# Retention and gated MLP on one core: smaller, paced loads, one mask product per first chunk, and another written order

## The chip, the cores and the metric

The kernel runs on one core of one Trainium2 chip. The time is that of the core on the device, in microseconds (us), from one execution of the whole program; the figure given for a kernel is the median of several executions. A core has a matrix engine (TensorE, PE in the profile, with its weight loads as PEld), a vector engine (VectorE, DVE), an activation engine (ScalarE, ACT), a general engine (GpSimd, POOL) and a sequencer for transfers (SyncE, SP). Each runs its own list of instructions in order and waits on the others by semaphores. Sixteen DMA engines move data between the chip's main memory (HBM) and the core's on-chip memory (SBUF); the matrix engine writes its products into a second on-chip memory (PSUM).

## The reference

There are 4 batches, 8 heads, 768 tokens and 64 dimensions per head. The first half is a retention layer, in which a state per head decays with every token:

```python
gamma = 1.0 - 2.0 ** (-5.0 - np.arange(H, dtype=np.float32))
for t in range(S):
    state = gamma[None, :, None, None] * state + np.einsum('bhd,bhe->bhde', k[:, :, t], v[:, :, t])
    y[:, :, t] = scale * np.einsum('bhd,bhde->bhe', q[:, :, t], state)
```

Its output, with the heads side by side (512 columns), is `x` of the second half, in which a causal convolution of 5 taps gives a gate:

```python
for k in range(K):
    gate_pre += conv_w[k][None, None, :] * xp[:, k:k + S, :]
gate = 1.0 / (1.0 + np.exp(-gate_pre))
val = x @ w_val
return (gate * val @ w_out).astype(np.float32)
```

The two weight matrices and the taps come in as 64-bit numbers, which the kernel turns into 32-bit ones itself.

## The kernel before

**Tiling.** The tokens are cut into 6 chunks of 128. A "visit" is one chunk of one batch, so there are 24, numbered `g`, with the 4 batches of a chunk in a row: visits 0 to 3 are the first chunk. The input of a visit is one block of 1 MB in four parts of 0.25 MB: part 0 the queries by dimension, part 1 the keys by dimension, part 2 the values by token, part 3 the keys by token. `load(g, part)` (L322) brings a block, or some of its parts, into one of four buffers (`LB`, L22), named `att` in the trace. A line of one partition has 2 KB for each part.

**The first chunk** (visits 0 to 3) needs no state from earlier. For each visit PE makes the scores (`first_scores`, L357, letter `s`), DVE multiplies them with a mask table (`first_mask`, L393), PE multiplies the masked scores with the values (`first_y`, L436, letter `y`), DVE scales the result into `x` (`evac`, L501). ACT then rounds `x` to `xh` (L512) and POOL makes the rest `xl` (L516). The two mask tables (one for each half `x` of the heads) are made once, by two DVE and two ACT instructions (`first_table`, L379), from `small_sb`, a block of 68 KB. Separately the keys by token are scaled on POOL (`decay`, L335, whose tile is `att` too) and PE adds the visit to the state (`first_state`, L456, letter `z`, tile `z_ps`). **Later visits** have a head (`head`, L460, letter `h`, only for visit 4) and a body (`attention`, letter `v`), in which POOL scales the values, and PE makes scores, outputs and state.

**The MLP.** For each chunk there are four value tiles (letter `V`): 12 matmuls of 512 columns (`val`, L604), as every number is a rounded part and a rest, and three of the four products are kept. Beside each runs a convolution: one tap on ACT (L593), four on DVE (L595), a sigmoid on ACT, the product with the gate on DVE (L625), a rounding on ACT (L632) and a rest on POOL (L636). Then come four output tiles (letter `O`): 12 matmuls (`outp`, L638), a copy on ACT and a store. Value tile and output tile share two PSUM banks, `mm`.

**The weights.** There are eight blocks of 0.5 MB (`load_w`, L527, tile `wst`, four buffers). Each is turned into 32-bit numbers by five instructions: two on ACT (L544, L563), two on DVE (L548, L554), one on POOL (L567). It is then split into a rounded part by ACT (L577) and a rest by POOL (L581; `wvl` for the value weights, `wol` for the output weights). Blocks 0 to 3 belong to the value tiles 0 to 3 of every chunk, blocks 4 to 7 to the output tiles, each of which needs all four.

**What sets the order.** The kernel describes its work as steps with a due time, an engine, an estimated cost and what they read and write. `plan` (L76) walks these steps through a small model of the engines and writes every engine's list of instructions in the order in which the model would start them: at each moment, of the steps that are ready for a free engine, the one with the lowest rank. The due times come from the strings `LOADS` (L687: what SP loads first, in order) and `WORK` (L690: the order of the letters above). So a letter's place in `WORK` is a priority, not its place in PE's list. While PE would be idle ahead of the first value tile, `plan` puts matmuls on zeros into its list (`filler`, L671); they write the bank `ye`, into which `first_y` writes too. Loads all go through SP's queue, in the order in which the model issues them; stores go through ACT's. In the model a load lands 2.7 us per MB after the load ahead of it.

Of the kernel before, what the change touches and what calls it, by code (L numbers as in the profile page):

```python
# [7 lines left out]
F32 = mybir.dt.float32  # L8
F32R = mybir.dt.float32r
# [243 lines left out]
def tile_retention_gated_mlp(  # L253
# [21 lines left out]
    mlp = ctx.enter_context(tc.tile_pool(name="mlp", bufs=2))  # L275
# [23 lines left out]
    sy = ps_y.tile([P, 2, 512], F32, name="sy")  # L299
# [1 line left out]
    ye = ps_m[0].tile([P, 2, 512], F32, name="ye")  # L301


    masks = [
        mlp.tile([P, 512], F32, name="o_sb")[:, 0:384].rearrange("p (j k t) -> p j k t", j=2, t=HALF)
        for x in range(2)
    ]

    steps = []

    def at(due, engine, cost, reads, writes, fn, *args):
        steps.append(Step(due, engine, cost, list(reads), list(writes), fn, args))
        return steps[-1]
# [5 lines left out]

    tiles, us, snaps, xs, xh, xl, decs, pos_ps = {}, {}, {}, {}, {}, {}, {0: base}, []  # L320

    def load(g, part=slice(0, 4)):  # L322
        b, c = chunks[g]
        if g not in tiles:
            tiles[g] = loads.tile([P, 4, 2, 2, P], F32, name="att")
        nc.sync.dma_start(out=tiles[g][:, part], in_=att[b * NCH + c, :, part])

    def get(dst, src, engine=nc.scalar):
        engine.dma_start(out=dst, in_=src)
# [49 lines left out]
    def first_table(x, part):  # L379


        vd = vd_sb[:, 0, 4 * x:4 * x + 4].rearrange("p (j s) -> p j s", s=2)
        if part == 0:
            nc.vector.tensor_tensor(
                masks[x][:, :, 0:3:2],
                vd.unsqueeze(3).broadcast_to([P, 2, 2, HALF]),
                tri_sb.unsqueeze(1).unsqueeze(1).broadcast_to([P, 2, 2, HALF]),
                op=ALU.mult,
            )
        else:  # L390
            nc.scalar.copy(masks[x][:, :, 1], vd[:, :, 0].unsqueeze(2).broadcast_to([P, 2, HALF]))

    def first_mask(g, x):  # L393
        if x == 0:
            us[g] = mlp.tile([P, 768], F32, name="u", bufs=2).rearrange("p (x j k t) -> p x j k t", x=2, j=2, t=HALF)
        nc.vector.tensor_tensor(  # L396
            us[g][:, x],
            sy[:, x, 0:384].rearrange("p (j k t) -> p j k t", j=2, t=HALF),
            masks[x],
            op=ALU.mult,  # L400
        )

# [108 lines left out]
    def round_x(n, b):  # L511
        if b == 0:  # L512
            xh[n] = mlp.tile([P, NPAIR, B, P], F32R, name="xh", bufs=XS)
        nc.scalar.copy(xh[n][:, :, b], xs[n][:, :, b, HALO:])  # L514

    def rest_x(n, b):  # L516
        if b == 0:
            xl[n] = mlp.tile([P, NPAIR, B, P], F32R, name="xl", bufs=XS)
        nc.gpsimd.tensor_tensor(  # L519
# [5 lines left out]
    raws, cvt = {}, {}  # L525

    def load_w(n):  # L527
        raws[n] = stage.tile([P, 512, 2], I32, name="wst", bufs=WB)
        src = w64[n // 4, n % 4].bitcast(I32).rearrange("p (n two) -> p n two", two=2)
        nc.sync.dma_start(out=raws[n], in_=src)  # L530

    def high(n):
        return raws[n][:, :, 1]
# [143 lines left out]
    def first_sigmoid():  # L677
# [22 lines left out]
    first_u = {}  # L700

    def first_scores_at(t, g):

        decay_at(t, g)
        sc, first_u[g] = Slot("sc", 1), Slot("u", 2)
        at(t, "PE", 0.5, [("att", g % LB, "qk"), "early"], [sc], first_scores, g).small = 32
        steps[-1].wide = 1.5
        for x in range(2):
            masked = [("mask", x, 0), ("mask", x, 1), sc]
            at(t + 0.02 + 0.01 * x, "DVE", (0.555, 0.475), masked + [first_u[g]] * x, [first_u[g], ("fu", g, x)][x:], first_mask, g, x)  # L710

# [13 lines left out]
    def decay_at(t, g):  # L725
        at(t, "POOL", TIMES["decay"], ["small"], [("att", g % LB, "kn" if g < B else "vk")], decay, g)
# [75 lines left out]
    def load_w_at(t, n):  # L802
        at(t, "DMA", 0.4, [], [wsts[n]], load_w, n).mb = 0.5
# [10 lines left out]
    def split(n, b, t):  # L814
        if b == 0:
            parts[n] = Slot("xh", XS), Slot("xl", XS)
        h, l = parts[n]
        x = [xbufs[n], ("x", n, b)]
        at(t, "ACT", TIMES["ACT"], x, [h, ("xh", n, b)], round_x, n, b)
        at(t + 0.1, "POOL", TIMES["POOL"], x + [h, ("xh", n, b)], [l, ("xl", n, b)], rest_x, n, b)  # L820

    def val_tile(n, m, t):
        bank = Slot("mm", 2)
        gate_of = gates[n, m]
        for i in range(3 * NPAIR):
# [37 lines left out]
    at(0.2, "DVE", 0.25, [], [xbufs[0]] + [("x", 0, i) for i in range(B)], new_x, 0)  # L863
    for p, (kind, n) in enumerate(LOADS):
        t = 0.1 * p
        if kind == "t":
            at(t, "DMA", 0.4, [], ["small"], get, small_sb, small, nc.sync).mb = 0.2
        elif kind == "a":
            load_at(t, n)
        elif kind == "q":  # L870
            at(t, "DMA", 0.4, [], [("att", 0, "qk")], load, 0, slice(0, 2)).mb = 0.5
        elif kind == "v":
            at(t, "DMA", 0.4, [], [("att", 0, "vk"), ("att", 0, "kn")], load, 0, slice(2, 4)).mb = 0.5
        else:
            load_w_at(t, n)
    for x in range(2):
        at(0.3 + 0.01 * x, "DVE", (0.42, 0.35), ["small"], [("mask", x, 0)], first_table, x, 0)
        at(0.32 + 0.01 * x, "ACT", (0.25, 0.2), ["small"], [("mask", x, 1)], first_table, x, 1)
# [8 lines left out]
    for what in WORK:  # L887
        i = now[what]
        now[what] += 1
        n, m = divmod(i, NPAIR)  # L890
# [4 lines left out]
        elif what == "s":  # L895
            t = max(t, 6.0 + CHUNK * i)
# [119 lines left out]
```

## Time and profile before

| | us |
|---|---|
| median of 3 runs | 213.45 (213.23 to 213.98) |
| the profiled execution | 213.34 |
| its span, first to last instruction | 211.5 |

The span is what the views of the trace divide up; the profiled execution is 1.84 us longer than it. "Busy" counts the time in which an engine has at least one instruction under way. Matmuls overlap one another, so a busy PE is not one at its peak. In the lists of the trace a row gives an engine, a line of the kernel, the tile written and the tiles read, how many instructions were merged, and in brackets how long the engine stood idle before it and which engine's work ended that. The chain of waits is followed back from the last instruction: at each step to the work that released it. The list of transfers gives for each group the size and the time from its issue to its landing.

### The profile page before, as it was taken

The numbers are of one execution on the slowest core, as the hardware profiler recorded it, in microseconds if no ns is written. First come the engines' busy times: TensorE is split into PE (matmuls) and PEld (weight loads), VectorE is DVE, ScalarE is ACT, GpSimd is POOL, SyncE is SP. The second block draws the span as 40 slices with busy tenths as digits, with TensorE's granted clock in tenths as the row PEclk, the third lists the DMA queues.
The fourth block names the chain that finished last, engine by engine and source line by source line (L and its number), as shares of the span: only waits on it lengthen the run. The fifth ranks groups of instructions, "written<-read, shape, count | busy, mean of one in ns | idle before, by whom it ended". The sixth has DMA issues, their size and how long they took to land.

```text
span 211.5 us, 7837 instructions
## 1 busy us (share of the span) xinstructions
PE 202.0 (96%) x3500; PEld 160.1 (76%) x3500; DVE 125.3 (59%) x193; ACT 109.7 (52%) x237; POOL 106.0 (50%) x93
## 2 busy tenths in 40 slices
PE   8976799999999999999999999999999999999993
PEld 3655578876787887888888887877777788888883
DVE  0467799994889322799589813499505599211000
ACT  2377657974793533964686334455345445311321
POOL 0279987899953773538565336242044624202200
PEclk9999999999999999999999999999999999999999
DMA  6999995647656703866352715521110010121122
GB/s 196 395 418 412 417 373 198 228 181 229 270 203 198 277 29 110 293 234 268 124 225 108 262 38 206 181 116 50 53 53 3 3 50 0 51 100 51 50 101 99
DMA packets 8677, 36.24 MB, mean 171 GB/s; under 512 B 1090, under 2 KB 1474, under 8 KB 5700
## 3 DMA queue, kind: packets, MB, share of 16 engines
q1 hardware_dynamic: 4896, 29.43, 37.5%
q10 hardware_dynamic: 3748, 6.32, 7.9%
q8 instruction: 27, 0.44, 0.9%
q14 instruction: 6, 0.05, 0.1%
HBM read 29.46 MB, written 6.29 MB: 169 GB/s over the span
## 4 chain that ended last, share of the span: by engine, by line
PE 79%; POOL 6%; ACT 2%; DVE 2%; issue 1%; DMA 1%; ACTq 0%; DVEq 0%
PE mm L610 31%; PE mm L644 29%; PE sy L424 9%; PE sy L350 4%; PE z_ps L408 3%; POOL wol L581 2%; POOL top L567 2%; POOL gvl L636 1%; PE ye L672 1%; DMA out_dram<-o_sb 1%; DVE u L396 1%; DVE x L504 1%; PE ye L441 0%; ACT o_sb L654 0%; PE sy L363 0%
## 5 line engine op out<-in xcount | busy, mean ns | idle before, releaser
L595 DVE SCALAR_TENSOR_TENSOR acc<-x,cw_sb,acc 128x512 f32<-128x512 f32 x96 | 68.1, 752 | 4.6 <-ACT acc L593 3.4
L636 POOL TENSOR_TENSOR gvl<-gate,gvh 128x512 fp32r<-128x512 f32 x24 | 30.9, 1288 | 45.0 <-ACT gvh L632 42.2
L519 POOL TENSOR_TENSOR xl<-x,xh 128x512 fp32r<-128x512 f32 x24 | 30.8, 1286 | 31.2 <-ACT xh L514 29.6
L644 PE MATMUL mm<-wol,gvh 128*128 128x512 f32 (+1 forms) x100 | 37.8, 390 | 0.5 <-POOL wol L581 0.5
L644 PE MATMUL mm<-woh,gvh 128*128 128x512 f32 (+1 forms) x100 | 37.6, 390 | 0.0
L644 PE MATMUL mm<-woh,gvl 128*128 128x512 f32 (+1 forms) x100 | 37.5, 389 | 0.0
L610 PE MATMUL mm<-xh,wvh 128*128 128x512 f32 x96 | 35.3, 399 | 0.0
L610 PE MATMUL mm<-xl,wvh 128*128 128x512 f32 x96 | 33.9, 406 | 0.0
L339 POOL TENSOR_TENSOR att<-att,small_sb 128x512 f32<-128x512 f32 x24 | 25.1, 1048 | 12.0 <-DMA small_sb<-in_small_dram 6.8
L372 DVE TENSOR_TENSOR u<-sy,small_sb 128x512 f32<-128x512 f32 x20 | 13.8, 688 | 24.9 <-PE sy L350 20.8
L625 DVE TENSOR_TENSOR gate<-mm,gate 128x512 f32<-128x512 f32 x24 | 16.4, 685 | 20.0 <-PE mm L610 20.0
L610 PE MATMUL mm<-xh,wvl 128*128 128x512 f32 x96 | 26.6, 397 | 0.0
L654 ACT COPY o_sb<-mm 128x512 f32<-128x512 f32 (+1 forms) x25 | 14.3, 571 | 23.0 <-PE mm L644 22.1
L632 ACT CAST gvh<-gate 128x512 fp32r<-128x512 f32 x24 | 14.8, 617 | 18.8 <-DVE gate L625 18.0
L644 PEld LDWEIGHTS mm<-wol,gvh 128*128 128x128 f32 x100 | 18.7, 188 | 5.3 <-POOL wol L581 1.4
L644 PEld LDWEIGHTS mm<-woh,gvh 128*128 128x128 f32 x100 | 18.7, 188 | 4.5 <-ACT woh L577 0.3
L644 PEld LDWEIGHTS mm<-woh,gvl 128*128 128x128 f32 x100 | 18.7, 188 | 4.1
L602 ACT ACTIVATE gate<-acc 128x512 f32<-128x512 f32 x24 | 14.4, 602 | 14.2 <-DVE acc L595 8.4
L610 PEld LDWEIGHTS mm<-xh,wvh 128*128 128x128 f32 x96 | 17.8, 188 | 4.4 <-ACT xh L514 0.2
L610 PEld LDWEIGHTS mm<-xh,wvl 128*128 128x128 f32 x96 | 17.9, 188 | 4.2
L610 PEld LDWEIGHTS mm<-xl,wvh 128*128 128x128 f32 x96 | 17.7, 188 | 4.4
L514 ACT CAST xh<-x 128x512 fp32r<-128x512 f32 x24 | 14.9, 620 | 9.5 <-DVE x L504 9.3
(49 smaller groups left out, 249.4 us busy)
## 6 DMA issues: line engine op xcount, KB each, us to landing
att<-in_att_dram SPq DMA_DIRECT2D x23, 1024.0 KB, 5.1
out_dram<-o_sb ACTq DMA_DIRECT2D x23, 256.0 KB, 2.1
wst<-in_w_dram SPq DMA_DIRECT2D x8, 512.0 KB, 10.2
att<-in_att_dram SPq DMA_DIRECT2D x2, 512.0 KB, 4.5
out_dram<-o_sb ACTq DMA_DIRECT2D x2, 128.0 KB, 1.7
small_sb<-in_small_dram SPq DMA_DIRECT2D x1, 68.0 KB, 5.4
cw_raw<-in_conv_w_dram ACTq DMA_DIRECT2D x1, 20.0 KB, 5.3
u<-in_pos_dram ACTq DMA_DIRECT2D x1, 5.0 KB
```

The source lines that it names most:

```text
L339: nc.gpsimd.tensor_tensor(v, v, vd_sb[:, c, :].unsqueeze(2).broadcast_to([P, 8, HALF]), op=ALU.mult)
L424: nc.tensor.matmul(sy[cols, h, off:off + HALF], lhsT=lhsT, rhs=rhs, start=start, stop=True, skip_group_check=True,)
L514: nc.scalar.copy(xh[n][:, :, b], xs[n][:, :, b, HALO:])
L519: nc.gpsimd.tensor_tensor(xl[n][:, :, b], xs[n][:, :, b, HALO:], xh[n][:, :, b].bitcast(F32), op=ALU.subtract)
L595: nc.vector.scalar_tensor_tensor(acc, x[:, :, k:k + P], cw_sb[:, m, k:k + 1], acc, op0=ALU.mult, op1=ALU.add,)
L602: nc.scalar.activation(gate[n, m], accs.pop((n, m)), AF.Sigmoid)
L610: nc.tensor.matmul(vps[n, m], lhsT=w[:, m, ct * P:(ct + 1) * P], rhs=xx[n][:, ct].rearrange("p b t -> p (b t)"), start=(i == 0), stop=(i = ...
L625: nc.vector.tensor_tensor(gv, vps.pop((n, m)), gv, op=ALU.mult)
L632: nc.scalar.copy(gvs[n, m][0], gate[n, m])
L636: engine.tensor_tensor(gvl, gate.pop((n, m)), gvh.bitcast(F32), op=ALU.subtract)
L644: nc.tensor.matmul(ops[n, b, cs.start][:, 0:cs.stop - cs.start], lhsT=gg[:, b * P:(b + 1) * P], rhs=w[:, ct, cs], start=(i == 0), stop=(i ...
L654: nc.scalar.copy(o_sb[:, 0:step], ops.pop((n, b, cs.start))[:, 0:step])
```

## The change

The change has five parts.

**Pieces.** A block of a later visit is loaded in two pieces of 0.5 MB, parts 0 and 1, then parts 2 and 3. For the first chunk, the list `LOADS` names pieces by letter: `q` is parts 0 and 1 (0.5 MB), `v` part 2 (0.25 MB), `k` part 3 (0.25 MB), `a` stands for `q` and then `v`.

**Pacing.** Each load of a block or of a weight passes through `paced`. It adds up the sizes of the loads issued before it, the latest first, its own among them, and lets the load wait for the landing of the first one that brings the sum over 1.5 MB.

**The order of the first loads.** The keys by token of visits 1 to 3 become pieces of their own; those of visit 0 are first of all, those of visits 1 and 2 come ahead of visit 1's other parts, and those of visit 3 just ahead of its other parts. `small_sb` moves up to the second place. A fifth weight block joins the list.

**One mask.** Both mask tables lie in one tile, which takes a buffer of the ring `xh` in place of two buffers of `o_sb`, and the mask product of a visit is one DVE instruction over 768 columns in place of two over 384. The tables' due time goes from 0.3 to 5.0.

**The written order.** `WORK` is another string. In it `z` of visits 0 and 1 stands ahead of `s` of visit 2, `y` of visit 2 ahead of `s` of visit 3, the head of visit 4 ahead of the first `V`, and all four `V` of the first chunk ahead of the first `v`.

```diff
-    masks = [
-        mlp.tile([P, 512], F32, name="o_sb")[:, 0:384].rearrange("p (j k t) -> p j k t", j=2, t=HALF)
-        for x in range(2)
-    ]
+    masks = mlp.tile([P, NPAIR, B, P], F32R, name="xh", bufs=XS).bitcast(F32)[:, 0:2].rearrange(
+        "p a b t -> p (a b t)"
+    )[:, 0:768].rearrange("p (x j k t) -> p x j k t", x=2, j=2, t=HALF)
...
+AHEAD = 1.5
...
+    under_way = []
+
+    def paced(dma, mb):
+
+        total = mb
+        for other, size in reversed(under_way):
+            total += size
+            if total > AHEAD:
+                tc.add_manual_dep(
+                    dma.ins, other.ins.name,
+                    mybir.DependencyInfo(mybir.DependencyClass.Sync, mybir.DependencyReason.DATA),
+                )
+                break
+        under_way.append((dma, mb))
...
-        nc.sync.dma_start(out=tiles[g][:, part], in_=att[b * NCH + c, :, part])
+        paced(nc.sync.dma_start(out=tiles[g][:, part], in_=att[b * NCH + c, :, part]), 0.25 * (part.stop - part.start))
...
-    def first_mask(g, x):
-        if x == 0:
-            us[g] = mlp.tile([P, 768], F32, name="u", bufs=2).rearrange("p (x j k t) -> p x j k t", x=2, j=2, t=HALF)
+    def first_mask(g):
+        us[g] = mlp.tile([P, 768], F32, name="u", bufs=2).rearrange("p (x j k t) -> p x j k t", x=2, j=2, t=HALF)
         nc.vector.tensor_tensor(
-            us[g][:, x],
-            sy[:, x, 0:384].rearrange("p (j k t) -> p j k t", j=2, t=HALF),
-            masks[x],
+            us[g].rearrange("p x j k t -> p x (j k t)"),
+            sy[:, :, 0:384],
+            masks.rearrange("p x j k t -> p x (j k t)"),
             op=ALU.mult,
         )
...
-    LOADS = (("v", 0), ("q", 0), ("t", 0), ("w", 0), ("a", 1), ("a", 2), ("w", 1), ("a", 3), ("w", 2), ("w", 3))
+    LOADS = (("k", 0), ("t", 0), ("q", 0), ("v", 0), ("w", 0), ("k", 1), ("k", 2), ("w", 1), ("a", 1), ("w", 2), ("a", 2), ("k", 3), ("a", 3), ("w", 3), ("w", 4))
...
     WORK = (
-        "spysyssyyVwzzwzhzVVvwwvVvOvOOvOVvvVVVOvvOVv"
-        "vVVvVvOOvOVVvOVvOVOOVvOVvvVvOVVVOOOVOVOOOOO"
+        "spysyzzsysyhwwVwVzzVVvvvOOvvOvVVvVvOVOOvVv"
+        "VOVvOvVvVvOOVvOVvOOvOVVVvVvvOvOVVOVOOOVOOOO"
     )
...
     def load_at(due, g):
-        at(due, "DMA", 0.4, [], [("att", g % LB, k) for k in ("qk", "vk", "kn")], load, g).mb = 1.0
+        at(due, "DMA", 0.4, [], [("att", g % LB, "qk")], load, g, slice(0, 2)).mb = 0.5
+        at(due + 0.0001, "DMA", 0.4, [], [("att", g % LB, k) for k in ("vk", "kn")], load, g, slice(2, 4)).mb = 0.5
+
+    def load_part_at(due, g, first, last):
+
+        keys = [("att", g % LB, k) for k, part in (("qk", 0), ("vk", 2), ("kn", 3)) if first <= part < last]
+        at(due, "DMA", 0.4, [], keys, load, g, slice(first, last)).mb = 0.25 * (last - first)
...
-        for x in range(2):
-            masked = [("mask", x, 0), ("mask", x, 1), sc]
-            at(t + 0.02 + 0.01 * x, "DVE", (0.555, 0.475), masked + [first_u[g]] * x, [first_u[g], ("fu", g, x)][x:], first_mask, g, x)
+        at(t + 0.02, "DVE", (0.955, 0.875), [mask_slot, sc] + [("mask", x, k) for x in range(2) for k in range(2)], [first_u[g]], first_mask, g)
...
-        elif kind == "a":
-            load_at(t, n)
-        elif kind == "q":
-            at(t, "DMA", 0.4, [], [("att", 0, "qk")], load, 0, slice(0, 2)).mb = 0.5
-        elif kind == "v":
-            at(t, "DMA", 0.4, [], [("att", 0, "vk"), ("att", 0, "kn")], load, 0, slice(2, 4)).mb = 0.5
+        elif kind in "aqvk":
+            for k, part in enumerate({"a": ((0, 2), (2, 3)), "q": ((0, 2),), "v": ((2, 3),), "k": ((3, 4),)}[kind]):
+                load_part_at(t + 0.001 * k, n, *part)
```

`load_w` calls `paced` in the same way, with 0.5 MB.

More of the change, by code (lines that the diff above doesn't have):

```diff
@@ L384, in first_table @@
             nc.vector.tensor_tensor(
-                masks[x][:, :, 0:3:2],
+                masks[:, x, :, 0:3:2],
                 vd.unsqueeze(3).broadcast_to([P, 2, 2, HALF]),
@@ L390, in first_table @@
         else:
-            nc.scalar.copy(masks[x][:, :, 1], vd[:, :, 0].unsqueeze(2).broadcast_to([P, 2, HALF]))
-    def first_mask(g, x):
-        if x == 0:
-            us[g] = mlp.tile([P, 768], F32, name="u", bufs=2).rearrange("p (x j k t) -> p x j k t", x=2, j=2, t=HALF)
+            nc.scalar.copy(masks[:, x, :, 1], vd[:, :, 0].unsqueeze(2).broadcast_to([P, 2, HALF]))
+    def first_mask(g):
+        us[g] = mlp.tile([P, 768], F32, name="u", bufs=2).rearrange("p (x j k t) -> p x j k t", x=2, j=2, t=HALF)
         nc.vector.tensor_tensor(
-            us[g][:, x],
-            sy[:, x, 0:384].rearrange("p (j k t) -> p j k t", j=2, t=HALF),
-            masks[x],
+            us[g].rearrange("p x j k t -> p x (j k t)"),
+            sy[:, :, 0:384],
+            masks.rearrange("p x j k t -> p x (j k t)"),
             op=ALU.mult,
@@ L529, in load_w @@
         src = w64[n // 4, n % 4].bitcast(I32).rearrange("p (n two) -> p n two", two=2)
-        nc.sync.dma_start(out=raws[n], in_=src)
+        paced(nc.sync.dma_start(out=raws[n], in_=src), 0.5)
     def high(n):
@@ L686, in tile_retention_gated_mlp @@
     CONV_LEAD, CHUNK = 7.0, 3.4
-    LOADS = (("v", 0), ("q", 0), ("t", 0), ("w", 0), ("a", 1), ("a", 2), ("w", 1), ("a", 3), ("w", 2), ("w", 3))
+    LOADS = (("k", 0), ("t", 0), ("q", 0), ("v", 0), ("w", 0), ("k", 1), ("k", 2), ("w", 1), ("a", 1), ("w", 2), ("a", 2), ("k", 3), ("a", 3), ("w", 3), ("w", 4))
     WORK = (
-        "spysyssyyVwzzwzhzVVvwwvVvOvOOvOVvvVVVOvvOVv"
-        "vVVvVvOOvOVVvOVvOVOOVvOVvvVvOVVVOOOVOVOOOOO"
+        "spysyzzsysyhwwVwVzzVVvvvOOvvOvVVvVvOVOOvVv"
+        "VOVvOVvVvVOOvVOvVOOvOVVVvVvvOvOVVOVOOOVOOOO"
     )
@@ L697, in load_at @@
     def load_at(due, g):
-        at(due, "DMA", 0.4, [], [("att", g % LB, k) for k in ("qk", "vk", "kn")], load, g).mb = 1.0
-    first_u = {}
+        at(due, "DMA", 0.4, [], [("att", g % LB, "qk")], load, g, slice(0, 2)).mb = 0.5
[3 more added lines that the diff above has]
+        at(due, "DMA", 0.4, [], keys, load, g, slice(first, last)).mb = 0.25 * (last - first)
+    first_u, mask_slot = {}, Slot("xh", XS)
     def first_scores_at(t, g):
@@ L707, in first_scores_at @@
         steps[-1].wide = 1.5
-        for x in range(2):
-            masked = [("mask", x, 0), ("mask", x, 1), sc]
-            at(t + 0.02 + 0.01 * x, "DVE", (0.555, 0.475), masked + [first_u[g]] * x, [first_u[g], ("fu", g, x)][x:], first_mask, g, x)
+        at(t + 0.02, "DVE", (0.955, 0.875), [mask_slot, sc] + [("mask", x, k) for x in range(2) for k in range(2)], [first_u[g]], first_mask, g)
     def first_y_at(t, g):
         y, vk = Slot("ye", 1), ("att", g % LB, "vk")
-        at(t, "PE", 0.5, [first_u[g], ("fu", g, 0), ("fu", g, 1), vk], [y, "early"], first_y, g).small = 32
+        at(t, "PE", 0.5, [first_u[g], vk], [y, "early"], first_y, g).small = 32
         steps[-1].wide = 1.5
@@ L876, in tile_retention_gated_mlp @@
     for x in range(2):
-        at(0.3 + 0.01 * x, "DVE", (0.42, 0.35), ["small"], [("mask", x, 0)], first_table, x, 0)
-        at(0.32 + 0.01 * x, "ACT", (0.25, 0.2), ["small"], [("mask", x, 1)], first_table, x, 1)
+        for k, (engine, cost) in enumerate((("DVE", (0.42, 0.35)), ("ACT", (0.25, 0.2)))):
+            first = x == k == 0
+            at(
+                5.0 + 0.01 * x + 0.02 * k, engine, cost, ["small"] + [mask_slot] * (not first),
+                [mask_slot] * first + [("mask", x, k)], first_table, x, k,
+            )
     early = [n for kind, n in LOADS if kind == "w"]
```

## The prediction, written before the changed kernel was run

> **What bounds the kernel now.** I read the page first: its engines, then the chain that ended last.
>
> ```profile
> PE 202.0 (96%) x3500; PEld 160.1 (76%) x3500; DVE 125.3 (59%) x193; ACT 109.7 (52%) x237; POOL 106.0 (50%) x93
> PE 79%; POOL 6%; ACT 2%; DVE 2%; issue 1%; DMA 1%; ACTq 0%; DVEq 0%
> ```
>
> PE is the bound as a whole. But an average hides stages, so next come the busy times by stretch, split at PE's first value matmul (26.4).
>
> ```profile
> 7.00:14.30 7.30, 6.38 (x171) 4.44 (x170) 5.46 (x11) 5.40 (x16) 3.71 (x4) 1.00 1.03 429
> 14.30:26.40 12.10, 8.70 (x251) 6.72 (x247) 8.70 (x15) 8.23 (x14) 12.07 (x11) 1.00 1.01 412
> 26.40:39.30 12.90, 12.90 (x239) 10.17 (x239) 12.64 (x21) 9.05 (x20) 10.24 (x9) 1.00 0.75 271
> 26.40:205.70 179.30, 178.33 (x3053) 143.66 (x3050) 110.98 (x168) 93.28 (x204) 89.99 (x75) 1.00 0.40 145
> ```
>
> The columns are the length, then PE, PEld, DVE, ACT, POOL, the clock, the DMA share and GB/s. After 26.4 PE is busy for 178.33 of 179.30 us: what remains is a fixed amount of matmul work, and the end is the start of the value matmuls plus that work. Before 26.4 it is not: PE has gaps and runs fillers, the DMA engines are full (1.01 to 1.03), and POOL works through all of 14.3 to 26.4. So the question is what sets 26.4. The chain in order of time shows it:
>
> ```profile
> 18.71 0.94 PE sy L363 x32
> 19.67 0.56 DVE u L396
> 20.23 0.62 DVE acc L548
> 20.88 0.56 DVE x L504
> 21.48 1.14 PE ye L672 x4
> 22.62 1.06 PE ye L441 x26
> 23.70 0.70 DVE x L504
> 24.44 1.14 PE ye L672 x4
> 25.58 0.62 PE sy L350 x32
> 26.20 0.23 PE z_ps L408 x16
> 26.44 3.46 PE mm L610 x14
> 29.89 0.62 PE z_ps L408 x32
> ```
>
> This is visit 3. Between its scores and its outputs stand a weight step (L548), the scaling of visit 2's outputs (L504) and four fillers, which wait for that scaling because they write the same bank. Then come fillers and the head of visit 4 ahead of the first value matmul. The two sets of rows for SP's queue and for landings give the arrivals:
>
> ```profile
> 0.74 0.85 SPq L326 DMA_DIRECT2D att<-in_att_dram  x2
> 2.10 0.65 SPq L530 DMA_DIRECT2D wst<-in_w_dram  x1
> 4.66 0.33 SPq L326 DMA_DIRECT2D att<-in_att_dram  x1
> 10.67 0.33 SPq L326 DMA_DIRECT2D att<-in_att_dram  x1
> ```
>
> ```profile
> att<-in_att_dram SPq DMA_DIRECT2D x1, 512.0 KB, 3.9
> wst<-in_w_dram SPq DMA_DIRECT2D x1, 512.0 KB, 6.3
> att<-in_att_dram SPq DMA_DIRECT2D x1, 1024.0 KB, 13.2
> att<-in_att_dram SPq DMA_DIRECT2D x1, 1024.0 KB, 12.5
> ```
>
> The rows answer, in turn, to the first piece of visit 0, weight 0, visit 3 and visit 4. The first piece lands at 0.74 + 3.9 = 4.6, weight 0 at 2.10 + 6.3 = 8.4, visit 3 at 4.66 + 13.2 = 17.9, visit 4 at 10.67 + 12.5 = 23.2. Visit 3's scores begin 0.8 after its data, and the first value matmul 8.5 after them.
>
> **The change part by part.**
>
> *Arrival of the last first-chunk scores.* From weight 0 to visit 3 the queue holds visits 1 and 2, weight 1 and visit 3: 3.5 MB in 9.5 us, or 2.71 us per MB. At the 429 GB/s of 7.0 to 14.3 it is 2.44. After the change, the first five transfers (keys, `small_sb`, queries, values, weight 0) hold the same bytes as before's first four, so I leave 8.4. From there to parts 0 and 1 of visit 3 are 0.25 + 0.25 + 0.5 + 0.75 + 0.5 + 0.75 + 0.25 + 0.5 = 3.75 MB: 17.55 at the one rate, 18.6 at the other. I take 2.6 us per MB, between them, so 18.15. The order alone thus brings the last scores 0.25 later than before, not earlier.
>
> *Pacing.* The order in which bytes are asked for is the same with or without the wait, so I put pacing itself at nothing. It can gain: today all up to visit 3 is issued by 4.7, when 0.5 MB of its 5 has landed, so the piece that is needed may share the engines with later ones; the gap between the two rates above bounds that at 3.75 x 0.27 = 1.0 us. It can lose if the queue runs dry (a rival, below). Behind each waiting load on SP stand only other loads. In the later stages loads wait for PE, not for landings, and the pieces cost nothing.
>
> *From the scores to the first value matmul.* The new order puts `y` of visit 2 ahead of `s` of visit 3, so its scaling is out of the way, and visit 3 pays its own chain: scores 0.94, mask, outputs 1.06, scaling 0.70, rounding.
>
> ```profile
> L396 DVE TENSOR_TENSOR u<-sy,o_sb 128x384 f32<-128x384 f32 x8 | 4.2, 550 | 1.5 <-PE sy L363 1.5
> L372 DVE TENSOR_TENSOR u<-sy,small_sb 128x512 f32<-128x512 f32 x20 | 13.8, 688 | 24.9 <-PE sy L350 20.8 <-ACT snap L419 4.1
> 24.42 0.69 ACT L593 ACTIVATE acc<-x,cw_sb 128x512 f32<-128x512 f32 x1 [1.20 <-DVE x L504]
> 25.05 0.60 ACT L514 CAST xh<-x 128x512 fp32r<-128x512 f32 x1
> ```
>
> The mask of 768 columns is not in the trace. Below, one of 512 takes 0.69; above, two of 384 take 1.10. 128 columns more cost 0.138, so 768 make 0.69 + 0.28 = 0.97: I take that. Merging saves about 0.1 and holds nothing up, since the outputs need both halves anyway. With a rounding of 0.60 the chain is 0.94 + 0.97 + 1.06 + 0.70 + 0.60 = 4.27; five handovers at 0.04, as in the chain, make 0.2; and I allow one foreign instruction in an engine's queue, as the tap of 24.42 stands ahead of the rounding now: 0.65. That is 5.1, and the first value matmul starts at 18.15 + 5.1 = 23.25, 3.15 earlier than 26.4. Without the foreign instruction it would be 22.6; with two and a filler of 0.3, 24.2.
>
> *What moves across that start.* The head of visit 4 was ahead of it (0.62 + 0.23); its block now comes behind weights 3 and perhaps 4, so I count it behind: +0.85. `z` of visit 3 was behind (0.62). In `WORK` both `z` of visits 2 and 3 come after the second `V`, but their keys come early, and a list that starts whatever is ready may use PE's gaps for them. Both ahead: +0.85 - 0.62 = +0.23. Both behind: +0.85 + 0.47 = +1.3. I take +0.6.
>
> *POOL, the next bound.* A start 2.5 us earlier is worth nothing if the output weights are ready as late as now.
>
> ```profile
> POOL att L339 <- DMA att<-in_att_dram: 2.5, 1, 2.5
> POOL wvl L581 <- ACT wvh L577: 1.3, 2, 1.1
> POOL top L567 <- ACT gate L602: 0.8, 1, 0.8
> POOL wol L581 <- ACT woh L577: 0.5, 1, 0.5
> POOL xl L519 <- ACT xh L514: 0.5, 1, 0.5
> POOL top L567 <- DVE top L554: 0.4, 1, 0.4
> 7.21 1.21 POOL L339 TENSOR_TENSOR att<-att,small_sb 128x512 f32<-128x512 f32 x1 [6.77 <-DMA small_sb<-in_small_dram]
> 51.51 1.28 POOL L581 TENSOR_TENSOR wol<-top,woh 128x512 fp32r<-128x512 f32 x1
> ```
>
> From 7.2 to 52.8 POOL waits 6.0 us in all, so its work up to the last `wol` is 39.6. It starts when `small_sb` and visit 0's keys are there. They now stand first, with 0.32 MB: about 4.6 at best, as the first 0.5 MB now, and 8.4, where weight 0 lands, at worst; I take 5.2, near the former, as less is ahead. The keys of visits 1 and 2 land by 8.4 + 0.5 x 2.6 = 9.7, so the wait of 2.5 for keys goes. If the other 3.5 us stay, POOL is done at 5.2 + 39.6 + 3.5 = 48.3, or 4.5 earlier, more than PE's 2.5. So POOL does not take the gain, with 2 us to spare. The fifth weight block in the first list helps: nothing on SP stands between it and its issue but pacing.
>
> *The masks' new place* costs nothing: the ring `xh` has two buffers, and the one of the masks is next needed by the first `v`, four value tiles (11.2 us) after the last mask product. *The tail* keeps its last four output tiles, at 0.
>
> *The sum*, against the profiled execution: 213.34 - 3.15 + 0.6 = 210.8. That execution stands 0.1 below the median of the runs shown, which is inside their spread.
>
> **The rivals.**
>
> *DVE takes the place of the loads.* All four `V` now stand in a row ahead of the first `v`.
>
> ```profile
> 25.69 4.83 DVE L595 SCALAR_TENSOR_TENSOR acc<-x,cw_sb,acc 128x512 f32<-128x512 f32 x7
> 178.01 6.99 PE mm L644 x30
> ```
>
> A tap is 0.69 (4.83 / 7), four with the gate product of the same length 3.45; 12 matmuls on PE are 2.80 (6.99 x 12 / 30). DVE falls back 0.65 per tile, and it is full already (12.64 of 12.90). For it speaks that each value tile beyond the second needs a bank that a gate product frees. Against it: the visits that follow cost PE more than DVE, and DVE starts earlier too. At most 2.6 is lost; I price it at 1.6: 212.4.
>
> *The queue runs dry.* The first 0.5 MB took 3.9 us, of which its bytes are 1.25 at 2.5 us per MB, so 2.65 are fixed. When a wait ends, 0.75 to 1.0 MB is still queued, 1.9 to 2.5 us. Two waits ahead of visit 3's scores find 0.75 (gap 0.75 each), four find 1.0 (0.15 each): 2.1 in all, and 212.9. Against it: in a running queue part of the fixed time is hidden. The Trainium skill, "DMA: Bandwidth & Descriptors", "Rules for kernel authors", asks for transfers of 1 MiB or more for full bandwidth, and its section "Bandwidth" gives 341 GB/s for one of 1 MB. By that figure, an estimate, the 3.75 MB take 11.5 us instead of 9.75, and the time would be 212.5; no run here yet shows small pieces alone, and the queue of mixed sizes above ran at 429.
>
> *The head holds the first value tile, and the kernel is slower.* `WORK` puts `h` ahead of `V`. If PE's list does too, the first value matmul waits for visit 4: 2.25 MB behind visit 3's scores (its values, weights 3 and 4, its own block), so 18.15 + 5.85 = 24.0 at the middle rate, or 8.4 + 6.0 x 2.71 = 24.7 at the slow one. Then come 1.04 of POOL, perhaps behind a rest of 1.29, and 0.85 of PE: the tile starts at 25.9 to 27.9. With `z` of visit 3 ahead (-0.62) that is 212.2 to 214.2, with both `z` behind (+0.47) 213.3 to 215.3; it turns slower once the tile starts later than 27.0 in the first case, 25.9 in the second. In the model of the planner as written, visit 4 would have to be ready before the tile for this. I price it at 214.4.
>
> **How the numbers follow.** The forecast (210.8, within 209.3 and 211.9) has 0.55; better than 209.3, with pacing gaining its full 1.0 and no foreign instruction, 0.05; DVE 0.18; the dry queue 0.12; the head 0.10. The range reaches from 209.3 to 213.6, which leaves the head's time and the best case out. This kernel's measurement tells 0.3% (0.64 us) from no change. Faster: 0.60, 0.15 of DVE's case and 0.02 of the dry queue's, so 0.77. Same: 0.03, 0.07 of the dry queue's and 0.02 of the head's, so 0.12. Slower: 0.03 of the dry queue's, should its gaps be longer, and 0.08 of the head's, so 0.11.
>
> **What would show it.** Right: visit 3's parts 0 and 1 land between 17.5 and 18.6; its scores follow within 0.3; the first L610 matmul starts near 23.3; POOL's last `wol` ends by 49; PE is busy without a gap over 1 us after that. Wrong: gaps in the DMA share before 20; L610 waiting for `gate` or `acc`; the head's L350 ahead of the first L610 with a wait for POOL's `att`; a last `wol` still at 52.

## The result: slower, 226.45 us against 213.5

| | before | after |
|---|---|---|
| median (lowest to highest), 4 executions each | 213.5 (213.23 to 213.98) | 226.45 (225.6 to 227.62) |
| the profiled execution | 213.34 | 225.6 |
| its span | 211.5 | 223.8 |

The ratio is 1.059, with a 95% interval from 1.054 to 1.064. The forecast was 210.8, with a range from 209.3 to 213.6: wrong in sign, and far outside. Ratios and intervals, here and below, leave out executions that lay over 1.5% above the fastest of the same kernel, while the medians count them. (In the diff above, the second line of the new `WORK` is not that of the kernel, which reads `VOVvOVvVvVOOvVOvVOOvOVVVvVvvOvOVVOVOOOVOOOO`.)

The page of the kernel after, its engines and its chain:

```profile
PE 204.7 (91%) x3492; PEld 162.2 (72%) x3492; DVE 123.8 (55%) x189; ACT 110.0 (49%) x237; POOL 106.0 (47%) x93
PE 76%; DMA 14%; POOL 3%; DVE 2%; issue 2%; ACT 1%; SPq 1%; ACTq 0%; POOLq 0%
```

All engines do almost the same work as before, but transfers, 1% of the chain before, are now 14%. The busy times by stretch say where. First the kernel after, then the kernel before; columns as above, the last one GB/s.

```profile
7.00:26.40 19.40, 13.93 (x326) 10.27 (x315) 10.23 (x16) 10.63 (x25) 12.19 (x11) 0.82 0.87 276
26.40:40.00 13.60, 10.61 (x141) 8.15 (x142) 9.28 (x15) 7.62 (x15) 10.89 (x10) 0.87 0.66 225
40.00:60.00 20.00, 14.64 (x411) 11.46 (x409) 13.08 (x22) 10.54 (x23) 11.11 (x10) 0.91 0.73 246
```

```profile
7.00:26.40 19.40, 15.08 (x418) 11.16 (x417) 14.16 (x25) 13.63 (x30) 15.78 (x15) 1.00 1.02 418
26.40:40.00 13.60, 13.60 (x286) 10.87 (x286) 13.34 (x22) 9.54 (x22) 10.94 (x10) 1.00 0.76 281
40.00:60.00 20.00, 19.48 (x492) 15.26 (x485) 15.84 (x25) 14.84 (x36) 19.58 (x17) 1.00 0.59 206
```

Three things to see. In 7 to 26.4 the rate falls from 418 to 276 GB/s, while the DMA share falls only from 1.02 to 0.87: the share counts engines that have something under way, so it hides most of a rate that is a third lower. From 40 to 60, where before PE had 0.52 us of idle time, it has 5.36. And the granted clock, 1.00 in every stretch before, is below 1 in all three.

The list of transfers in 7 to 26.4, first after, then before (the last number is the median from issue to landing):

```profile
att<-in_att_dram SPq DMA_DIRECT2D x5, 512.0 KB, 5.9
wst<-in_w_dram SPq DMA_DIRECT2D x4, 512.0 KB, 5.6
```

```profile
wst<-in_w_dram SPq DMA_DIRECT2D x6, 512.0 KB, 10.5
att<-in_att_dram SPq DMA_DIRECT2D x3, 1024.0 KB, 11.8
```

A single transfer lands sooner than before, and still fewer bytes land in all. The chain of the kernel after, in order of time (start, length, what), shows why:

```profile
2.58 5.90 DMA wst<-in_w_dram
...
8.54 5.59 DMA att<-in_att_dram
...
14.52 5.60 DMA att<-in_att_dram
...
20.14 5.32 DMA wst<-in_w_dram
...
25.52 6.11 DMA wst<-in_w_dram
```

From 2.6 to 31.6 the end of the kernel hangs on nothing but landings: each transfer is issued as soon as the one before it in the chain has landed. The five trips from issue to landing last 5.70 us in the mean, and at 276 GB/s, the number of the window, 1.57 million bytes are then under way: the limit of 1.5 MB, as 1 MB is 1.049 million bytes here. The same trips at before's 418 GB/s would need 2.4 million bytes.

What this does to PE, in the list of PE's instructions of the kernel after (in brackets the idle time before each and what ended it):

```profile
22.61 0.90 PE L378 MATMUL sy<-att 64*64 64x128 f32 x32 [0.79 <-DMA att<-in_att_dram]
28.12 1.77 PE L624 MATMUL mm<-xh,wvh 128*128 128x512 f32 x4 [2.64 <-ACT xh L528]
38.93 1.20 PE L624 MATMUL mm<-xh,wvh 128*128 128x512 f32 x4 [1.27 <-DVE gate L639]
50.14 0.46 PE L422 MATMUL z_ps<-att 64*64 64x64 f32 x16 [2.23 <-POOL att L354]
53.26 0.50 PE L658 MATMUL mm<-woh,gvh 128*128 128x512 f32 x1 [0.84 <-ACT woh L591]
56.05 0.79 PE L658 MATMUL mm<-wol,gvh 128*128 128x512 f32 x1 [2.29 <-POOL wol L595]
```

Visit 3's scores begin at 22.61 instead of 18.71, and the first value matmul at 28.12 instead of 26.37. The last three waits, 5.36 us together, are all the idle time of 40 to 60. The `wol` that PE waits for at 56.05 is only the second of four; the last one is ready at 64.2, not by 48.3, as POOL's list shows:

```profile
62.88 1.28 POOL L595 TENSOR_TENSOR wol<-top,woh 128x512 fp32r<-128x512 f32 x1
```

### The profile page after: what moved, and what is told of

It is laid out like the page before. It is cut to its first block, busy times and chain, and to the rows that moved or that the text cites. A ratio compares the mean times of both kernels' runs of the same rounds, so it can differ in the third digit from the quotient of the medians.

```text
span 223.8 us, 7858 instructions
## 1 busy us (share of the span) xinstructions
PE 204.7 (91%) x3492; PEld 162.2 (72%) x3492; DVE 123.8 (55%) x189; ACT 110.0 (49%) x237; POOL 106.0 (47%) x93
## 3 DMA queue, kind: packets, MB, share of 16 engines
HBM read 29.46 MB, written 6.29 MB: 160 GB/s over the span
## 4 chain that ended last, share of the span: by engine, by line
PE 76%; DMA 14%; POOL 3%; DVE 2%; issue 2%; ACT 1%; SPq 1%; ACTq 0%; POOLq 0%
PE mm L658 30%; PE mm L624 28%; PE sy L438 11%; DMA wst<-in_w_dram 8%; DMA att<-in_att_dram 5%; PE sy L365 4%; PE z_ps L422 3%; DVE acc L609 1%; POOL top L581 1%; POOL att L354 1%; DMA out_dram<-o_sb 1%; SPq L341 1%; POOL wol L595 1%; ACT o_sb L668 0%; DVE gate L639 0%
## 5 line engine op out<-in xcount | busy, mean ns | idle before, releaser
L609 DVE SCALAR_TENSOR_TENSOR acc<-x,cw_sb,acc 128x512 f32<-128x512 f32 x96 | 66.6, 750 | 3.9 <-ACT acc L607 3.6
L658 PE MATMUL mm<-woh,gvh 128*128 128x512 f32 (+1 forms) x100 | 38.1, 391 | 0.8 <-ACT woh L591 0.8
L658 PE MATMUL mm<-woh,gvl 128*128 128x512 f32 (+1 forms) x100 | 38.3, 395 | 0.0
L624 PE MATMUL mm<-xh,wvh 128*128 128x512 f32 x96 | 32.5, 405 | 3.9 <-ACT xh L528 2.6
L624 PE MATMUL mm<-xl,wvh 128*128 128x512 f32 x96 | 33.0, 406 | 0.0
L624 PE MATMUL mm<-xh,wvl 128*128 128x512 f32 x96 | 27.4, 406 | 0.0
L624 PEld LDWEIGHTS mm<-xh,wvl 128*128 128x128 f32 x96 | 18.5, 194 | 4.6
L518 DVE TENSOR_TENSOR x<-sy,dec 128x512 f32<-128x512 f32 x20 | 13.7, 683 | 13.1 <-PE sy L365 10.7
```

What stands on the lines that cost most here:

```text
L609: nc.vector.scalar_tensor_tensor(acc, x[:, :, k:k + P], cw_sb[:, m, k:k + 1], acc, op0=ALU.mult, op1=ALU.add,)
L624: nc.tensor.matmul(vps[n, m], lhsT=w[:, m, ct * P:(ct + 1) * P], rhs=xx[n][:, ct].rearrange("p b t -> p (b t)"), start=(i == 0), stop=(i = ...
L658: nc.tensor.matmul(ops[n, b, cs.start][:, 0:cs.stop - cs.start], lhsT=gg[:, b * P:(b + 1) * P], rhs=w[:, ct, cs], start=(i == 0), stop=(i ...
```

## The experiments

Three theories stood after the result; their letters are those of the expectations below. **A: the limit.** 1.5 MB under way can't fill the engines; without it the time comes back. **B: the pieces.** Transfers of 0.25 and 0.5 MB are slow in themselves. **C: the written order.** `WORK` and a full DVE cost the time. The first runs led to **D: the order of SP's list.** A later block is now two steps, so its first piece can be planned ahead of weights and other loads and then hold up all that stands behind it on SP. E, F and G are about `WORK` and the first loads, and H is that PE's clock costs a part. Each kernel was timed beside the kernel before. The results together:

| label | limit | blocks of later visits | else | median us | ratio (95%) |
|---|---|---|---|---|---|
| (after) | 1.5 MB | two steps | | 226.45 | 1.054 to 1.064 |
| no_cap | none | two steps | | 221.61 | 1.030 to 1.042 |
| cap3 | 3.0 MB | two steps | | 222.08 | 1.032 to 1.046 |
| cap_whole | 1.5 MB | one step | | 222.38 | 1.032 to 1.047 |
| cap2_whole | 2.0 MB | one step | | 219.38 | 1.023 to 1.031 |
| no_cap_whole | none | one step | | 216.01 | 1.005 to 1.010 |
| whole_old_work | none | one step | `WORK` of before | 217.66 | 1.013 to 1.021 |
| old_cut | none | one step | rest as before | 214.02 | 0.998 to 1.003 |
| old_halves | none | two steps | rest as before | 224.13 | 1.041 to 1.056 |
| old_paced | 1.5 MB | one piece of 1 MB | rest as before | 228.96 | 1.062 to 1.080 |
| mask_only | none | one piece of 1 MB | before, with the one mask | 214.42 | 1.001 to 1.007 |
| after_fillers | 1.5 MB | two steps | 14 fillers more | 228.45 | 1.061 to 1.076 |
| whole_fillers | none | one step | 14 fillers more | 221.46 | 1.025 to 1.041 |

### The limit

```diff
-AHEAD = 1.5
+AHEAD = 1000.0
```

That is no_cap; cap3 has 3.0 instead. In old_paced the loads of the kernel before, in its own pieces of 1 MB and 0.5 MB, pass through `paced` with 1.5.

> The changed kernel with the limit raised so far that no load ever waits for another's landing; pieces, first order, mask and written order stay. Theory A (the wait holds the queue to 1.5 MB per 5.5 us, about 280 GB/s): the rate of 7 to 26 us goes back to about 415 GB/s, visit 3's scores come near 18.2 us instead of 22.6, the first value matmul near 23.3, and the time is 210 to 212. Theory B (pieces of 0.25 and 0.5 MB with their shorter lines are slow): the rate stays near 280 GB/s and the time near 226. Theory C (the written order and the full DVE cost the time, the loads only come with it): the rate goes back, but PE still stands idle between 35 and 60 us, and the time is 220 or more.

> The changed kernel with a limit of 3.0 MB in place of 1.5. Theory A: 3.1 MB in 5.5 us would be 570 GB/s, more than the queue moves, so nothing is held up: within 1 us of the kernel with no limit. Theory B or C: no change from 226. If the time from issue to landing grows with the limit, it lies between the two.

> The kernel before, with its own pieces (1 MB per later visit), order and masks, and only the wait with 1.5 MB added. Theory A: the rate of 7 to 26 us falls from 418 to 300 GB/s or less, visit 3 lands at 21 or later instead of 17.9, and the time is 217 to 226. Theory B and C: 213 to 214.

The windows of no_cap, of cap3 and of old_paced, in this order:

```profile
7.00:26.40 19.40, 13.33 (x319) 10.02 (x311) 11.89 (x18) 12.62 (x29) 14.20 (x13) 0.91 1.02 393
...
40.00:60.00 20.00, 14.78 (x308) 10.98 (x309) 9.54 (x15) 8.26 (x18) 14.74 (x13) 0.74 0.61 214
```

```profile
7.00:26.40 19.40, 14.33 (x337) 11.10 (x334) 11.96 (x19) 13.03 (x30) 14.74 (x14) 0.91 1.03 390
```

```profile
7.00:26.40 19.40, 12.35 (x329) 9.51 (x328) 9.54 (x18) 9.04 (x23) 10.42 (x10) 0.92 0.70 249
```

With no limit, or with 3.0 MB, the rate is back at 390 to 393. The limit costs 1.059 - 1.036 = 2.3% of 213.5, so 5.0 us in this kernel, and 7.1% or 15 us in the kernel before: there only one block of 1 MB fits under 1.5 MB beside a weight, and the rate is 249. Theory A holds for the rate, but it explains less than half: by it no_cap would have taken 210 to 212 us, and it took 221.61. Without a limit 3.6% are left, and PE still loses 5.2 us in 40 to 60. (old_paced, at 228.96, is also slower than the 217 to 226 that were expected.)

### The blocked list

```diff
     def load_at(due, g):
-        at(due, "DMA", 0.4, [], [("att", g % LB, "qk")], load, g, slice(0, 2)).mb = 0.5
-        at(due + 0.0001, "DMA", 0.4, [], [("att", g % LB, k) for k in ("vk", "kn")], load, g, slice(2, 4)).mb = 0.5
+        at(due, "DMA", 0.4, [], [("att", g % LB, k) for k in ("qk", "vk", "kn")], load_both, g).mb = 1.0
+
+    def load_both(g):
+        load(g, slice(0, 2))
+        load(g, slice(2, 4))
```

This is what "one step" means in the table: the same two pieces, but planned together. no_cap_whole has it with no limit, cap_whole with 1.5 MB. In the other direction, old_halves gives the kernel before the two steps, and old_cut gives it the pieces alone:

```diff
-        nc.sync.dma_start(out=tiles[g][:, part], in_=att[b * NCH + c, :, part])
+        for first in range(part.start, part.stop, 2):
+            cut = slice(first, first + 2)
+            nc.sync.dma_start(out=tiles[g][:, cut], in_=att[b * NCH + c, :, cut])
```

> The kernel before with the blocks of later visits loaded in two pieces of 0.5 MB and no wait. Theory A and C: 213 to 214.5. Theory B: 217 or more, as each 4 KB line would cost more per byte than one of 8 KB.

> The changed kernel without the limit, and with one step per later block, which waits for all readers of its buffer and then issues both pieces of 0.5 MB. Theory D (SP's queue is blocked: the first piece of visit 6 stands ahead of weights 6 and 7 in SP's list, and cannot be issued before the state matmul of visit 2, because the buffer is handed over as a whole): SP no longer stands still from 20 to 33 us, weights 6 and 7 land near 30 instead of 39 to 41, PE keeps its work in 40 to 60 us, and the time is 210 to 215. Theory E (the order of WORK is itself worse, whatever SP does): PE still loses 5 us or more in 40 to 60, and the time stays at 219 or more.

> The same with the limit of 1.5 MB back: the changed kernel with only the blocked queue mended. Theory A (the limit costs on its own): the rate of 7 to 26 us is 275 to 300 GB/s again, the first value matmul comes near 28, and the time is 219 to 226. If the limit costs only through the blocked queue, it is within 2 us of the run without it.

> The kernel before with each load of a later block issued as two transfers of 0.5 MB from one step, so that every engine's list stays as it was. Theory D: the pieces themselves cost nothing, 213 to 214.5. Theory B (each small transfer costs the queue time): 217 or more, like the run with halves as steps of their own (224).

What theory D says can be read in SP's own list. First no_cap, then the row of its waits, then no_cap_whole:

```profile
20.07 13.49 SPq L341 DMA_DIRECT2D att<-in_att_dram  x2
33.66 0.37 SPq L544 DMA_DIRECT2D wst<-in_w_dram  x1
...
35.68 0.37 SPq L544 DMA_DIRECT2D wst<-in_w_dram  x1
```

```profile
SPq L341 <- PE z_ps L422: 12.8, 1, 12.8
```

```profile
20.25 4.20 SPq L544 DMA_DIRECT2D wst<-in_w_dram  x2
31.80 11.40 SPq L341 DMA_DIRECT2D att<-in_att_dram  x8
```

In no_cap SP stands for 12.8 us at a block load that waits for PE's `z_ps`, and weights 6 and 7 are issued at 33.66 and 35.68. In no_cap_whole they go out from 20.25, in before from 22.56, and the block loads that wait come behind them. In the kernel after, with its limit, the same load holds weight 6:

```profile
31.65 5.97 SPq L341 DMA_DIRECT2D att<-in_att_dram  x2
37.73 0.37 SPq L544 DMA_DIRECT2D wst<-in_w_dram  x1
```

The load in question is the first piece of visit 6. In the planner's model that piece needs only parts 0 and 1 of its buffer, which visit 2's scores have read; in the kernel as built the buffer `att` is handed over as a whole, and visit 2's state product reads it last. PE does that product behind the second value tile, as its list shows for no_cap. Below it stand visit 3's scores and the first value matmul of no_cap_whole:

```profile
25.59 1.20 PE L624 MATMUL mm<-xh,wvh 128*128 128x512 f32 x4 [1.46 <-ACT xh L528]
...
32.44 1.16 PE L422 MATMUL z_ps<-att 64*64 64x64 f32 x64
```

```profile
19.63 0.85 PE L378 MATMUL sy<-att 64*64 64x128 f32 x32
...
24.17 1.19 PE L624 MATMUL mm<-xh,wvh 128*128 128x512 f32 x4 [1.71 <-ACT xh L528]
```

What PE then waits for goes back to a further load in that row. In SP's list as the planner wrote it, behind the first piece of visit 6 stand weight 6, the first piece of visit 7, weight 7, and only then the second piece of visit 6. That one goes out at 36.10 in no_cap and at 42.80 in the kernel after, and takes 8.1 and 6.1 us to land, so it lands at 44.2 and 48.9. POOL stands idle in its list until just then (no_cap, then the kernel after; the trace names no releaser):

```profile
44.35 1.04 POOL L354 TENSOR_TENSOR att<-att,small_sb 128x512 f32<-128x512 f32 x1 [8.17 <-issue]
```

```profile
49.04 1.04 POOL L354 TENSOR_TENSOR att<-att,small_sb 128x512 f32<-128x512 f32 x1 [7.98 <-issue]
```

In the kernel after, PE's waits of 50.14, 53.26 and 56.05 are for this step of POOL and for the weight steps behind it.

The window of 40 to 60, once the blocks are one step (no_cap_whole), and that of old_cut and of cap_whole in 7 to 26.4:

```profile
40.00:60.00 20.00, 18.88 (x559) 14.70 (x561) 11.91 (x20) 13.75 (x34) 18.91 (x17) 1.00 0.68 221
```

```profile
7.00:26.40 19.40, 14.69 (x340) 10.53 (x332) 11.68 (x22) 11.57 (x27) 14.51 (x14) 0.85 1.03 409
```

```profile
7.00:26.40 19.40, 14.90 (x322) 11.39 (x314) 10.18 (x16) 10.45 (x25) 12.31 (x11) 0.74 0.91 292
```

Two steps cost 1.036 - 1.008 = 2.8%, or 6.0 us, without a limit, and 1.059 - 1.039 = 2.0%, or 4.3 us, with one; in the kernel before, old_halves, 4.8%. The limit costs 3.15%, or 6.7 us, once the list is mended. old_halves, at 224.13, is in the range that its expectation gave to theory B, but old_cut tells the pieces from their place in the list: the same sizes from one step have a ratio of 1.000, and its traced execution (217.62 us, at a granted clock of 0.85 in this window) moves 409 GB/s. So the pieces as such cost nothing, B is out, and theory D holds beside theory A. In no_cap_whole PE is busy for 18.88 of the 20 us from 40 to 60 under the new `WORK`, so C and E are not what costs the time there. Its median of 216.01 is still 1 us above the range that was expected by D.

### How much under way is enough

cap2_whole is cap_whole with 2.0 MB.

> The changed kernel with the queue of SP mended (one step per later block) and a limit of 2.0 MB. Theory A in numbers: with 1.5 MB the queue carries 1.57 MB per 5.5 us; with 2.0 MB it carries 2.1 MB per 5.5 us, 380 GB/s in 7 to 26 us instead of 295, and the time lies between the 215 of no limit and the 222 of 1.5 MB, near 217. If the time to landing grows with what is under way, the rate stays nearer 300 and the time nearer 222.

```profile
7.00:26.40 19.40, 14.21 (x330) 10.72 (x330) 11.17 (x17) 11.31 (x26) 12.79 (x12) 0.82 0.96 333
```

From 1.5 to 2.0 MB the rate goes from 292 to 333 and the time from 222.4 to 219.4; 2.1 million bytes at 333 GB/s is a trip of 6.3 us (its pieces took a median of 5.7 to 6.6). The expectation of 380 GB/s kept the trip at 5.5 us; it grows with what is under way, so the rate comes out in between. At 3.0 MB (390) the limit hardly costs rate any more.

### The written order and the mask alone

whole_old_work puts the `WORK` of before into no_cap_whole, less its first `w`, since the first five weights are in `LOADS` already. mask_only is the kernel before with the one mask, its place in the ring `xh` and its due time.

> No limit, the queue of SP mended, and the string WORK of the kernel before (its first w left out, since five weights stand in the first list). Theory F (what is left of the loss, 215 against 213.5, is the new string): 212 to 213.5, with PE's losses after the first value matmul as in the kernel before. Theory G (it is the pieces of the first list or the mask, that is, the arrivals): 214.5 to 216.

> The kernel before with only the merged mask, its tile in the ring xh and its due time of 5.0; loads and order strings are those of before. If the mask is neutral, as forecast: 213 to 214. If it costs (one buffer of xh held, or the lists of the engines shift), 215 or more.

With the old string the kernel is slower than with the new one, a ratio of 1.017 against 1.008, outside of both expectations, so going back to the old string does not win back what is left of the loss. The mask alone gives 1.004: neutral to a little slower. (Its ten executions had a mean granted clock of 0.973 to 0.992, so the clock may be this difference.) Its one instruction took, in the list of DVE's instructions of the kernel after:

```profile
7.61 0.96 DVE L410 TENSOR_TENSOR u<-sy,xh 128x768 f32<-128x768 f32 x1 [1.26 <-PE sy L378]
```

### PE's clock

The windows had shown a granted clock below 1. Cut at the places where it changes, the kernel after gives this (the stretch between, at 1.00, is left out):

```profile
7.00:11.44 4.44, 3.31 (x95) 2.21 (x85) 2.93 (x6) 2.88 (x9) 1.04 (x1) 1.00 0.90 260
11.44:18.27 6.83, 5.67 (x100) 4.42 (x99) 2.53 (x4) 3.79 (x10) 5.75 (x6) 0.50 0.79 281
...
28.51:31.92 3.41, 3.41 (x10) 2.55 (x8) 0.00 (x0) 0.27 (x1) 2.37 (x3) 0.50 0.63 225
```

A third stretch lies at 55.81 to 59.23. In the 3.41 us from 28.51 PE is busy throughout, and that is the beginning of the first value tile. So a further theory, H, was that a good part of the loss is the half clock, and that matmuls on zeros, which keep PE busy, win it back cheaply. after_fillers and whole_fillers (this one from no_cap_whole) put two fillers ahead of the scores of visits 1 to 3 and two behind those of visits 0 to 3:

```diff
+        if step.fn is first_scores and step.args[0] > 0:
+            filler(); filler()
         step.fn(*step.args)
+        if step.fn is first_scores:
+            filler(); filler()
```

> The changed kernel, with the limit and the blocked queue as they are, and 14 more fillers on PE: two behind each first_scores and two ahead of those of visits 1 to 3; every engine's order is the same otherwise. Theory H (a part of the loss is PE's clock, which the trace shows at half speed for 13.6 us in three stretches after short gaps): the stretch at 11 to 18 us goes, the granted clock of 7 to 20 us is 1.0, and 1.5 to 3.5 us of the 13 are won; the stretches near 28 and 56, where PE waits longer, stay. If the clock costs nothing, as PE waits for loads anyway: 226 within 0.7.

> The same 14 fillers in the kernel with no limit and the queue mended. Its executions lay between 214.5 and 220.8. Theory H: that spread is the clock, and with it at 1.0 all executions come within 214 to 216, none faster than 213.4. If the fillers delay the first chunk, whose gaps are short here: 215.5 to 217.

The first window of whole_fillers:

```profile
7.00:26.40 19.40, 16.66 (x315) 12.20 (x306) 9.31 (x15) 9.11 (x23) 10.95 (x10) 1.00 1.02 394
```

The clock is at 1.00 there, and the kernel is slower all the same, a ratio of 1.033 against 1.008: the fillers stand in PE's list ahead of the work, and the first value matmul comes at 29.46 instead of 24.17. after_fillers also gets its clock of 1.00 in 7 to 26.4, and is 2 us slower than the kernel after instead of 1.5 to 3.5 faster. The theory fell as far as a cheap gain goes. What the clock alone costs in the kernel after stays unmeasured. In the kernel before, 6.8 us at half clock went with 1.8 us (last section); at that rate the 13.7 us of the three stretches would be worth some 3.6 us of the 13, an estimate.

No version that was run beats the kernel before.

## Why the prediction was wrong, point by point

**What bounds it: right in the main.** The end was taken as the start of the value matmuls plus a fixed amount of work. In no_cap_whole, where neither fault is left, the first value matmul is 2.2 us earlier than before, yet the span is 1.2 longer (212.7 against 211.5, from its traced execution, at 214.53 us the fastest of ten). Of those 3.4 us, 1.3 are PE work that moved behind the start. Another 1.65 are idle PE time, as the window of no_cap_whole from 26.4 to 205.7 shows against that of before:

```profile
26.40:205.70 179.30, 176.68 (x3113) 142.03 (x3112) 109.77 (x168) 93.69 (x201) 88.91 (x75) 1.00 0.44 147
```

PE is idle there for 2.62 us, before for 0.97. Three waits that before does not have make up the difference, for DVE's gate product and its scaling and for ACT's copy of an output tile:

```profile
32.59 1.19 PE L624 MATMUL mm<-xh,wvh 128*128 128x512 f32 x4 [0.41 <-DVE gate L639]
45.52 0.69 PE L438 MATMUL sy<-u,att 64*64 64x64 f32 x32 [0.73 <-DVE x L518]
65.01 0.50 PE L624 MATMUL mm<-xh,wvh 128*128 128x512 f32 x1 [0.52 <-ACT o_sb L668]
```

So the forecast held for the early part, while the "fixed amount" let in new waits; half a microsecond isn't accounted for.

**Pacing at nothing: the step that failed first.** "The order in which bytes are asked for is the same with or without the wait" is true and beside the point: the wait changes how many bytes are under way. The rival "the queue runs dry" had the mechanism, with a chance of 0.12 and a price of 2.1 us; by the runs it is 5.0 us here and 6.7 with the mended list. Its term was mis-sized in two places. It took 3.9 us from issue to landing, from the very first piece, which had no transfer ahead of it; the median trips in the kernel after were 5.3 to 5.9. And it let a queue that still holds 0.75 to 1.0 MB run at full speed until it is empty. The trace of before held the better estimate: the rate times the trip is what is under way, so before's 418 GB/s at a trip of only 3.9 us would already need 1.63 million bytes, more than the limit's 1.57. Why a trip takes 5.7 us under the limit, and not 3.9, no run separates.

The Trainium skill, "DMA: Bandwidth & Descriptors", "Rules for kernel authors", asks for 1 MiB or more in one transfer for full bandwidth. The trace disagrees for the sizes of this kernel: pieces of 0.5 MB moved 409 GB/s in old_cut, as long as enough of them were under way, and old_paced, with its blocks of 1 MB, moved 249, where they were not.

**"In the later stages loads wait for PE, not for landings, and the pieces cost nothing": the step that failed second.** Its last part is right of the size (old_cut). But a piece as a step of its own has a place of its own in SP's list. "Behind each waiting load on SP stand only other loads" was meant as a comfort, and it was the fault: those other loads were weights 6 and 7 and, behind them, the second piece of visit 6, for which POOL and then PE stood idle. That was worth 4.3 us here, 6.0 without the limit, and no rival had it.

**Arrival of visit 3 at 18.15 and first value matmul at 23.25: right in kind, once the limit and the list are mended.** In no_cap_whole the scores begin at 19.63 and the first value matmul at 24.17, so 1.5 and 0.9 later than forecast. The chain between them took 4.54 there, and 5.51 in the kernel after, against a forecast of 5.1. The one foreign instruction of the forecast is there: a weight step of DVE (L562) stands ahead of the scaling of visit 3. In the kernel after, DVE stands idle ahead of it for 1.59 us, until 26.13, since its weight lands at 25.46 only. As it stood, the kernel had 22.61 and 28.12.

**The one mask: right**, 0.96 measured, 0.97 forecast.

**What moves across the start: at its upper bound.** Both `z` and the head came behind the start of the first value tile (+1.3 instead of +0.6).

**POOL, "done by 48.3": wrong.** The last `wol` ends at 64.2 in the kernel after, since POOL's data were late. It ends at 51.2 in no_cap_whole, against 52.8 before, so POOL gained less there than PE's start did; PE waits 0.28 us for a `wol` all the same, against 0.52 before.

**The rival "DVE takes the place of the loads"** shows in small: the third value tile waits for its gate product, 0.41 us in no_cap_whole and 1.27 in the kernel after. The rival takes DVE for full, but in the kernel after it stood idle from 28.51 to 31.92 (0.00 busy in that window), until the work on a weight that landed at 31.63. **"The head holds the first value tile"** is not what the trace shows: the first value matmul waits for the rounding `xh`, and the head comes behind it.

**The sum of the difference.** The span grew by 12.3 us. From the trace of the kernel after: first value matmul 1.75 later (28.12 against 26.37), 1.3 of work moved behind it, 4.84 more idle PE time in 40 to 60, 1.27 in 26.4 to 40 beyond the later start (13.60 - 10.61 - 1.72, the wait for the gate product), and two half-clock stretches after the start. Those stretches can cost at most half of their 3.41 us each, 3.4 in all, which would make 12.6. This split is worked out from one execution; the shares of limit and list are measured.

**What stays open.** The trace names the three waits behind the 1.65 us of later idle PE time in no_cap_whole, but which part of the change lets them in, no run says. Nor was the clock's own share in the kernel after isolated. Without the limit and with the list mended, 0.8% (0.5 to 1.0%) is left to the kernel before.

## What to carry to other kernels

A limit on the bytes under way is a limit on the rate: it has to exceed the full rate times the time from issue to landing. That time is not the one of a first, lone transfer, and it grows with what is under way (a median of 5.3 to 5.9 us at 1.5 MB, 5.7 to 6.6 at 2.0, 10.5 to 11.8 in the kernel before, without a limit), so what is enough has to be tried: here 1.5 MB gave 276 to 292 GB/s, 2.0 gave 333, 3.0 was enough. A load that is split into steps gets a new place in an in-order queue; ask what stands behind it, and whether the buffer is really handed over in the units that the planner assumes. Read GB/s beside the DMA share, because here the share was still 0.87 when a third of the rate was gone.

## What the runs showed of the hardware

**PE's clock was at half for whole stretches, after short gaps.** In the kernel after these lasted 6.83, 3.41 and 3.42 us; the first began at 11.44, when PE had been idle for 1.13 us in all since 7.0 (4.44 - 3.31). But the gaps alone don't decide it. Up to this place PE does the same work in no_cap_whole, with the same gap of 1.08 us, and there the clock stayed at 1.00, though PE stood idle for 5.85 of the 19.40 us. The row behind the gap in the kernel after, then in no_cap_whole, and its window:

```profile
11.18 1.86 PE L686 MATMUL ye<-const-float32-0.0 128*128 128x256 f32 x4 [1.08 <-DVE x L518]
```

```profile
11.34 1.14 PE L686 MATMUL ye<-const-float32-0.0 128*128 128x256 f32 x4 [1.08 <-DVE x L518]
```

```profile
7.00:26.40 19.40, 13.55 (x340) 10.14 (x332) 12.23 (x19) 13.40 (x30) 15.57 (x14) 1.00 1.02 391
```

The same four matmuls take 1.86 us in the one and 1.14 in the other. What starts a stretch is not shown.

The Trainium skill, "TensorE: Matmul & The Clock Gate", "What's actually happening", describes a window of 3413 ns that runs freely; the lengths of the stretches agree with one and two of those. The Trainium skill, on the same page under "Why this matters for your kernels", asks for no gap over about 3 us; by that rule the gaps ahead of 11.44 would cost nothing, and the trace of the kernel after disagrees.

**The same list can meet it or miss it.** Beside the experiments the kernel before was executed 46 times. In 6 of these the mean granted clock was 0.984, which is 6.8 us at half clock, and the time 215.27 to 216.05; in the other 40 it was 0.996 to 1.000, and the time 213.17 to 213.99. The medians are 1.8 us apart. So a single execution of the same lists can stand 2 us off, and a difference of that size has to be read from several.
